# A planner's time for VectorE's instructions made a fourteenth longer, for ScalarE's a twenty-fifth

## The chip, the core and the metric

The kernel runs on one core of a Trainium2 chip. Its time is what one execution takes on the device, in microseconds; several executions are timed, and their median counts. One more execution is recorded by the hardware profiler, and all rows below are from that one.

## What is computed

Three layers follow one another on 4 batches of 768 tokens with 384 channels. The first is a gated linear attention with 8 heads of 48 channels; the second a gated network whose gate is mixed over the tokens; the third turns the channels by angles, mixes the tokens with two more 768 x 768 matrices and ends with a product over the channels.

```python
# layer 1, for each batch and head: state is 48 x 48, f = sigmoid(f_logit)
state = f[t][:, None] * state + outer(k[t], v[t])
y[t] = q[t] @ state
# layer 2
h = gelu_tanh(x @ w_in)
u, v = h[..., :512], h[..., 512:]
v_n = (v - mean(v)) / sqrt(var(v) + 1e-06) * g_ln
v_s = einsum('ts,bsd->btd', w_sg, v_n) + b_sg[None, :, None]
x = x + (u * v_s) @ w_out
# layer 3
theta = x @ w_theta
y = einsum('ts,bsd->btd', w_tok_r, x * cos(theta)) + einsum('ts,bsd->btd', w_tok_i, x * sin(theta))
u = x + y
out = u + maximum(u @ w_ch, 0)
```

The weights arrive as 64-bit floats, which the kernel reads as pairs of 32-bit integers.

## The kernel before

**Numbers in two parts.** A product in full float32 precision is made of three: each factor is split in a high part (fp32r) and the rest, and high x high, high x low and low x high are summed in one PSUM bank (lines 783, 784 and 785 of one helper, so all products have these three lines). ScalarE writes the high part and VectorE subtracts it to make the low part: L802 and L803 for the activations, L792 and L793 for a gated tile, L446 and L447 for a weight. Four PSUM banks (mm_95 to mm_98) serve these products, two more the attention (at).

**Decodes.** A 64-bit weight tile is loaded by SyncE (L420) into one of two raw buffers, ScalarE takes the absolute value of its upper word (L432), VectorE assembles the 32-bit float in four steps (L433 to L436), L446 and L447 split it, into one single buffer wt, and GpSimd issues its store to a scratch in DRAM (L483, scratch<-wt). Only when that store has landed can the next L446 write wt. The 24 tiles of the third layer's token mix are decoded so during the earlier layers; later SyncE streams them back (L493, st<-scratch) into five buffers. The channel weight w_ch is decoded in three parts into wmid, stored by L483 and loaded by L475 (win<-scratch) into the place of the input weights.

**Order of the work.** Batch by batch, layer 2 runs with the attention of the next batch between its products; layer 3 follows, the last batch first. In layer 2 the v tiles come first (products into a bank, gelu L958, mean L963 and L964, square L967, then for three tiles the power L979 on GpSimd, the scaling L987 on ScalarE and its low part L991 on VectorE), then u (gelu L828), the spatial gating (24 products into four banks at once, evicted by L846, multiplied by u in L851, split by L792 and L793) and the projection with w_out, whose sum is added in L807. The attention of a half batch needs a gate's seeds for four pairs of heads: a memset on GpSimd (L568), a scan on VectorE, the logarithm L583 and the exponential L584 on ScalarE; then for each pair transposes (L628), copies, the scores and the state updates (L681, L686) and a copy of the result (L733), which GpSimd's L756 sends to the next layer's input. Each change between ScalarE's sets of functions (gelu; logarithm and exponential; sine) takes a table load (L312).

**The planner.** No order is written by hand: every instruction is first put into a list with its engine, a planned duration, what it reads and writes and a due time vt. The planner makes each due time the least of its own and of its successors' due times less the planned cost, lets the engines run in a simulation and takes on each the ready instruction that is due first. The instructions are then emitted in that order, and each engine keeps it on the chip. The foreground's due times advance with the products; the decodes' are set apart by constants (LATE_AT, LATE_STEP). A duration is a line in the number n of columns, v1 for most VectorE operations, a1 for ScalarE's, and every additional engine waited for adds WAIT2:

```python
    def v1(n):
        return 0.069 + n * 0.00104

    def a1(n):
        return 0.1 + n * 0.00081
```

Of the kernel before, what the change touches and what calls it, by code (L numbers as in the profile page):

```python
# [65 lines left out]
LOOK = 0.05  # L66
SWITCH = 2.0
WAIT2 = 0.065

TICK = 10.24 / 3  # L70
DMA_SLACK = 1.0
# [43 lines left out]
class Plan:  # L115
# [17 lines left out]
    def op(self, eng, dur, fn, r=(), w=(), wp=(), table=None, dma=0, vt=None, cols=None):  # L133
        o = Op()
        o.eng, o.dur, o.fn, o.table, o.dma = eng, dur, fn, table, dma
        o.vt, o.n = self.vt if vt is None else vt, len(self.ops)
        o.cols = dur * 2400 if cols is None else cols
        deps, o.need = set(), []
        for b in r:
            deps.update(b.writers)  # L140
        for b in w:
            deps.update(b.writers)
        for b in (*w, *wp):
            deps.update(b.readers)
        for b in r:
            b.readers.append(o)
        for b in w:
            b.writers, b.readers = [o], []
        for b in wp:
            b.writers = b.writers + [o]  # L150
        for b in (*r, *w, *wp):
            root = b.of or b
            if root.slots is not None:
                if root not in o.need:
                    o.need.append(root)
                if not root.acc or root.acc[-1] is not o:
                    root.acc.append(o)

        o.dur += WAIT2 * max(0, len({d.eng + str(bool(d.dma)) for d in deps if d.eng != eng or d.dma}) - 1) * (eng in ("DVE", "ACT"))
        o.deps, o.succ, o.left = deps, [], len(deps)  # L160
        for d in deps:
            d.succ.append(o)
        self.ops.append(o)
        return o
# [159 lines left out]
def body(tc, ctx, att, qkv, flog, w_in, g_ln, w_sgT, b_sg, w_out, w_theta, w_rT, w_iT, w_ch, out):  # L324
# [87 lines left out]
    def load_f32(pl, g, d, src, vt, background=False):  # L412

        n = src.shape[-1]
        get = lambda: d.t[:, :n]
        if src.dtype != I64:
            dma(pl, "SP", n * 512, lambda: nc.sync.dma_start(get(), src), w=[d], vt=vt - 3)
            return
        raw = pl.buf(g.raw if background else g.st, [P, 2 * TH], I32)
        dma(pl, "SP", n * 1024, lambda: nc.sync.dma_start(raw.t[:, : 2 * n], src.bitcast(I32)), [], [raw], vt=vt - 3)  # L420

        def bits():
            r = raw.t[:, : 2 * n].rearrange("p (n two) -> p n two", two=2)
            return r[:, :, 0], r[:, :, 1]

        def op(dur, fn, eng="DVE"):
            pl.op(eng, dur, fn, [raw], [d], vt=vt)

        V, iget = nc.vector, lambda: get().bitcast(I32)


        op(a1(n), lambda: nc.scalar.activation(get(), bits()[1].bitcast(F32), AF.Abs), "ACT")  # L432
        op(v2(n), lambda: V.tensor_scalar(get(), get(), TINY, None, ALU.max))  # L433
        op(v2(n), lambda: V.tensor_scalar(iget(), iget(), 3, 0x3FFFFFFF, ALU.logical_shift_left, ALU.bitwise_and))
        op(v1(n), lambda: V.scalar_tensor_tensor(iget(), bits()[1], -0x40000000, iget(), ALU.bitwise_and, ALU.bitwise_or))  # L435
        op(v1(n), lambda: V.scalar_tensor_tensor(iget(), bits()[0], 29, iget(), ALU.logical_shift_right, ALU.bitwise_or))  # L436
# [801 lines left out]
```

## Time and profile before

| what | us |
|---|---|
| median of 3 timed runs | 668.9 |
| lowest and highest | 667.99, 669.65 |
| the profiled execution | 673.68 |
| its span, first to last instruction | 671.8 |
| TensorE busy in it | 615.1 |
| VectorE, ScalarE, GpSimd busy | 445.8, 355.9, 107.9 |

The mean clock granted to TensorE in the profiled execution is 0.982 of full speed. Times inside the program are counted from the start of its span. An engine's idle time costs something only where another engine, in the end TensorE, waits for it.

### The profile page before, as it was taken

Reading aid. Unit: us, or ns where it says so; the run is one execution under the profiler, and the core shown is the slowest. Engines: PE = TensorE matmul, PEld = TensorE weight load, DVE = VectorE, ACT = ScalarE, POOL = GpSimd, SP = SyncE. Lnnn points to the kernel's source line nnn. Section 1 sums busy time; section 2 is a strip of 40 time slices with the busy share of each in tenths; the row PEclk is TensorE's granted clock in tenths of the full one; section 3 lists DMA queues with packets and bytes.
Section 4 is the critical chain, followed back from the end, with each engine's and each line's share of the span. In section 5 each row is a group of like instructions: output and inputs, shape, how many; then the busy total and the mean of one; then the engine's idle time right before and its main releaser. Section 6 shows DMA issues by size and latency. Waiting matters only on the chain.

```text
span 671.8 us, 15019 instructions
## 1 busy us (share of the span) xinstructions
PE 615.1 (92%) x5963; PEld 566.7 (84%) x5963; DVE 445.8 (66%) x1029; ACT 355.9 (53%) x752; POOL 107.9 (16%) x202
## 2 busy tenths in 40 slices
PE   9788588799999999999989988999999999999996
PEld 8677477688888797888979888889989998998995
DVE  6999677979779988788765667932481175148203
ACT  6759596757795548855357234820390065029200
POOL 2001332153431432512313010000000000000000
PEclk9999878999999999999989999999999999999998
DMA  8531853478547684555764857188628844860862
GB/s 326 206 95 62 323 176 122 121 254 281 179 127 238 219 296 160 167 183 191 255 220 147 268 179 252 49 300 295 209 84 272 254 162 144 257 211 24 256 190 77
DMA packets 49296, 131.50 MB, mean 196 GB/s; under 512 B 6816, under 2 KB 17248, under 8 KB 48960
## 3 DMA queue, kind: packets, MB, share of 16 engines
q1 hardware_dynamic: 38656, 88.95, 41.0%
q0 software_dynamic: 10560, 41.49, 17.8%
q8 instruction: 49, 0.80, 0.5%
q14 instruction: 31, 0.25, 0.1%
HBM read 100.93 MB, written 24.77 MB: 187 GB/s over the span
## 4 chain that ended last, share of the span: by engine, by line
PE 31%; DVE 24%; ACT 19%; DMA 14%; issue 9%; POOL 2%; SPq 0%; DVEq 0%; POOLq 0%; ACTq 0%
PE mm L783 10%; PE mm L785 10%; PE mm L784 10%; DMA raw<-in_w_iT 3%; DMA scratch<-wt 3%; DVE dt L435 2%; DMA xst<-y 2%; DMA dt<-in_w_sgT 2%; ACT ar L792 2%; DVE s L681 2%; DVE dt L436 2%; DVE ar L793 2%; ACT tmp L964 1%; ACT junk L967 1%; ACT tmp L958 1%
## 5 line engine op out<-in xcount | busy, mean ns | idle before, releaser
L783 PE MATMUL mm<-st,ar 128*128 128x384 f32 x480 | 165.3, 344 | 4.6 <-DVE xst L807 2.3
L785 PE MATMUL mm<-st,ar 128*128 128x384 f32 x480 | 161.3, 336 | 0.0
L784 PE MATMUL mm<-st,ar 128*128 128x384 f32 x480 | 161.2, 336 | 0.0
L802 ACT CAST x<-xst 128x384 fp32r<-128x384 f32 x72 | 36.7, 512 | 150.5 <-DVE xst L807 126.6
L807 DVE TENSOR_TENSOR xst<-xst,mm 128x384 f32<-128x384 f32 x48 | 25.8, 551 | 109.9 <-PE mm L785 109.8
L783 PEld LDWEIGHTS mm<-st,ar 128*128 128x128 f32 x480 | 90.5, 189 | 8.7 <-DVE xst L807 3.0
L784 PEld LDWEIGHTS mm<-st,ar 128*128 128x128 f32 x480 | 90.6, 189 | 0.3
L785 PEld LDWEIGHTS mm<-st,ar 128*128 128x128 f32 x480 | 90.5, 189 | 0.0
L783 PE MATMUL mm<-win,x 128*128 128x512 f32 (+1 forms) x144 | 56.0, 389 | 8.8 <-DVE tmp L846 4.0
L783 PE MATMUL mm<-x,win 128*128 128x384 f32 x168 | 58.9, 351 | 3.1 <-DVE tmp L846 1.8
L785 PE MATMUL mm<-x,win 128*128 128x384 f32 x168 | 56.8, 338 | 0.8 <-DVE win L447 0.8
L785 PE MATMUL mm<-win,x 128*128 128x512 f32 (+1 forms) x144 | 53.7, 373 | 3.8 <-DVE x L803 3.8
L784 PE MATMUL mm<-x,win 128*128 128x384 f32 x168 | 56.6, 337 | 0.0
L784 PE MATMUL mm<-win,x 128*128 128x512 f32 (+1 forms) x144 | 53.4, 371 | 0.1
L793 DVE TENSOR_TENSOR ar<-tmp,ar 128x384 fp32r<-128x384 f32 x80 | 41.2, 553 | 4.3 <-ACT ar L792 3.8
L792 ACT CAST ar<-tmp 128x384 fp32r<-128x384 f32 x80 | 37.7, 508 | 12.0 <-DVE tmp L851 11.1
L803 DVE TENSOR_TENSOR x<-xst,x 128x384 fp32r<-128x384 f32 x72 | 37.5, 553 | 4.4 <-ACT x L802 3.1
L783 PEld LDWEIGHTS mm<-win,x 128*128 128x128 f32 x144 | 27.4, 190 | 14.2 <-DVE tmp L846 5.3
L783 PE MATMUL mm<-ar,wout 128*128 128x384 f32 x96 | 34.6, 360 | 2.0 <-DVE tmp L898 1.8
L783 PEld LDWEIGHTS mm<-x,win 128*128 128x128 f32 x168 | 31.8, 189 | 5.1 <-DVE tmp L846 2.4
L756 POOL DMA_DIRECT2D xst<-y x60 | 30.8, 518 | 26.3 <-ACT y L733 17.1
L785 PEld LDWEIGHTS mm<-win,x 128*128 128x128 f32 x144 | 27.6, 191 | 7.4 <-DVE x L803 4.4
(146 smaller groups left out, 1238.4 us busy)
## 6 DMA issues: line engine op xcount, KB each, us to landing
st<-scratch SPq DMA_DIRECT2D x132, 384.0 KB, 3.8
qkv<-in_qkv POOLq DMA_DIRECT2D x24, 536.0 KB, 5.5
scratch<-wt POOLq DMA_DIRECT2D x24, 384.0 KB, 3.9
f<-in_flog POOLq DMA_DIRECT2D x6, 768.0 KB, 5.2
scratch<-st POOLq DMA_DIRECT2D x12, 384.0 KB, 6.8
raw<-in_w_rT SPq DMA_DIRECT2D x12, 384.0 KB, 4.1
raw<-in_w_iT SPq DMA_DIRECT2D x12, 384.0 KB, 4.9
out<-xst SPq DMA_DIRECT2D x24, 192.0 KB, 2.2
```

What stands on the lines that cost most here:

```text
L435: op(v1(n), lambda: V.scalar_tensor_tensor(iget(), bits()[1], -0x40000000, iget(), ALU.bitwise_and, ALU.bitwise_or))
L436: op(v1(n), lambda: V.scalar_tensor_tensor(iget(), bits()[0], 29, iget(), ALU.logical_shift_right, ALU.bitwise_or))
L681: pl.op("DVE", 0.16, lambda: V.tensor_add(s1(), s0(), U(c)), r=[ps, b0], w=[b1])
L756: lambda r0=r0, n=n, kc=kc, o=64 * j + off: q[yq].dma_start(xst.t[r0 : r0 + n, kc], y.t[o : o + n].rearrange("p i a t -> p (i a t)")),
L783: nc.tensor.matmul(o, h0, h1, start=start, stop=False)
L784: nc.tensor.matmul(o, h0, l1, start=False, stop=False)
L785: nc.tensor.matmul(o, l0, h1, start=False, stop=stop)
L792: pl.op("ACT", a1(n), lambda: nc.scalar.copy(tiles()[0], src.t[:, :n]), [src], [hi])
L793: pl.op("DVE", v1(n), lambda: V.tensor_sub(tiles()[1], src.t[:, :n], tiles()[0].bitcast(F32)), [src, hi], [lo])
L802: pl.op("ACT", a1(TH), lambda: nc.scalar.copy(X[hf][:, 0, k], T()), [src], [hi])
L803: pl.op("DVE", v1(TH), lambda: V.tensor_sub(X[hf][:, 1, k], T(), X[hf][:, 0, k].bitcast(F32)), [src, hi], [lo])
L807: pl.op("DVE", v1(TH), lambda: V.tensor_add(T(), T(), ps.t[:, :TH]), [ps], [xst[hf].parts[k]])
```

## The change

The planner multiplies every planned duration of VectorE by 1.07 and of ScalarE by 1.04. Nothing else is edited; the same operations are emitted, in another order on each engine.

```diff
 SWITCH = 2.0
 WAIT2 = 0.065
 
+
+SLOW = {"DVE": 1.07, "ACT": 1.04}
+
 TICK = 10.24 / 3
@@ -157,6 +160,7 @@
         o.dur += WAIT2 * max(0, len({d.eng + str(bool(d.dma)) for d in deps if d.eng != eng or d.dma}) - 1) * (eng in ("DVE", "ACT"))
+        o.dur *= SLOW.get(eng, 1.0)
         o.deps, o.succ, o.left = deps, [], len(deps)
```

Of VectorE's planned instructions 633 of 1016 stand elsewhere, by up to 61 places; of ScalarE's 359 of 689, of GpSimd's 84 of 193, of SyncE's 88 of 272. ScalarE's planned part holds 17 table loads, where it held 15. From line 70 on, the changed kernel's lines have numbers higher by 3, from line 160 on by 4: L846 is L850 there.

GpSimd during batch 1's first attention, 94 to 140 us. L979 is the power of layer 2's statistics, L568 the memset of the next half's seeds. Before:

```order
L491 DMA scratch_91<-st_1172 128x768
L963 TENSOR_SCALAR stat_875<-stat_875 128x1 x3
L539 DMA f_1265<-in_flog 128x1536
L979 TENSOR_TENSOR stat_875<-stat_875,mhalf 128x3
L568 MEMSET seed_1311 128x1536
L491 DMA scratch_91<-st_1294 128x768
```

After:

```order
L495 DMA scratch_91<-st_1186 128x768
L967 TENSOR_SCALAR stat_887<-stat_887 128x1 x3
L543 DMA f_1317<-in_flog 128x1536
L572 MEMSET seed_1330 128x1536
L983 TENSOR_TENSOR stat_887<-stat_887,mhalf 128x3
L495 DMA scratch_91<-st_1319 128x768
```

The power and the memset have changed places.

ScalarE during batch 3's attention in the middle of the run. L583 and L584 are the logarithm and the exponential of the seeds, L828 the gelu of u, L987 the scaling of three v tiles. Before:

```order
L828 ACTIVATE u_3820<-mm_97 128x384
L828 ACTIVATE u_3825<-mm_96 128x384
L312 ACT_TABLE_LOAD
L583 ACTIVATE seed_3469<-f_3491 128x1536
L733 COPY y_3881<-at_99 128x2x3x64
L691 ACTIVATE s_3865<-s_3865,bends 128x48 x2
L691 ACTIVATE carry_3902<-s_3865,bends 128x48
L584 ACTIVATE seed_3469<-seed_3469 128x1536
L312 ACT_TABLE_LOAD
L828 ACTIVATE u_3916<-mm_95 128x384
```

After:

```order
L832 ACTIVATE u_3767<-mm_96 128x384
L737 COPY y_3771<-at_100 128x2x3x64
L695 ACTIVATE s_3760<-s_3760,bends 128x48 x2
L316 ACT_TABLE_LOAD
L587 ACTIVATE seed_3537<-f_3553 128x1536
L991 ACTIVATE ar_0_3820<-tmp_3617,stat_3496 128x512
L991 ACTIVATE ar_0_3820<-tmp_3695,stat_3496 128x512
L991 ACTIVATE ar_0_3820<-tmp_3707,stat_3496 128x512
L695 ACTIVATE carry_3837<-s_3760,bends 128x48
L636 ACTIVATE kt_3842<-at_100 128x384
L316 ACT_TABLE_LOAD
L832 ACTIVATE u_3849<-mm_97 128x384
```

The three scalings, a transpose's copy (L632, now L636) and the gelus have come between the logarithm and the exponential, with a table load before and one after them; the exponential (L588) follows seven rows further down, behind one more load.

VectorE at the spatial gating of batch 2's second half, 335 to 348 us. L846 evicts one of its four banks, L851 and L793 multiply and split; L433 to L436 and L447 belong to a decode. L1101 belongs to the test of the decays. Before:

```order
L846 SCALAR_TENSOR_TENSOR tmp_4566<-mm_98,gcol,bbc 128x384
L851 TENSOR_TENSOR tmp_4566<-tmp_4566,u_4169 128x384
L793 TENSOR_TENSOR ar_0_4561<-tmp_4548,ar_0_4561 128x384
L447 TENSOR_TENSOR wt_4572<-dt_4323,wt_4572 128x384
L793 TENSOR_TENSOR ar_0_4561<-tmp_4566,ar_0_4561 128x384
L433 TENSOR_SCALAR dt_4584<-dt_4584 128x384
L434 TENSOR_SCALAR dt_4584<-dt_4584 128x384
L435 SCALAR_TENSOR_TENSOR dt_4584<-raw_4481,dt_4584 128x384
L436 SCALAR_TENSOR_TENSOR dt_4584<-raw_4481,dt_4584 128x384
L846 SCALAR_TENSOR_TENSOR tmp_4610<-mm_97,gcol,bbc 128x384
L1101 TENSOR_REDUCE lmin<-lps 1x1
L851 TENSOR_TENSOR tmp_4610<-tmp_4610,u_4196 128x384
```

After:

```order
L797 TENSOR_TENSOR ar_0_4563<-tmp_4546,ar_0_4563 128x384
L440 SCALAR_TENSOR_TENSOR dt_4540<-raw_4478,dt_4540 128x384
L850 SCALAR_TENSOR_TENSOR tmp_4580<-mm_96,gcol,bbc 128x384
L855 TENSOR_TENSOR tmp_4580<-tmp_4580,u_4163 128x384
L850 SCALAR_TENSOR_TENSOR tmp_4596<-mm_97,gcol,bbc 128x384
L850 SCALAR_TENSOR_TENSOR tmp_4604<-mm_98,gcol,bbc 128x384
L855 TENSOR_TENSOR tmp_4596<-tmp_4596,u_4179 128x384
L797 TENSOR_TENSOR ar_0_4563<-tmp_4580,ar_0_4563 128x384
L855 TENSOR_TENSOR tmp_4604<-tmp_4604,u_4266 128x384
L451 TENSOR_TENSOR wt_4578<-dt_4374,wt_4578 128x384
L797 TENSOR_TENSOR ar_0_4563<-tmp_4596,ar_0_4563 128x384
```

The second, third and fourth eviction now stand ahead of the decode's L447 (now L451), and its four steps come later still. At the next spatial gating, near 382 us, one L447 and four decode steps stand right before the four evictions in both orders.

SyncE loads the third part of w_ch five places later, behind four more stream loads L493, and on TensorE 57 products of the last batch's token mix stand ahead of the first product with w_ch, where there were 42.

## Rows read from the trace of the kernel before

**Rows 1.** Busy time of each engine in six stretches of the span, whole kernel.

```profile
core 0: us, PE busy (x) PEld busy (x) DVE busy (x) ACT busy (x) POOL busy (x), PEclk, DMA share, GB/s
0.00:94.00 94.00, 75.74 (x1116) 65.80 (x1117) 77.69 (x221) 68.08 (x152) 15.32 (x37) 0.93 0.55 191
94.00:140.00 46.00, 38.94 (x623) 33.42 (x622) 40.17 (x99) 28.69 (x58) 14.24 (x23) 0.96 0.45 141
140.00:341.00 201.00, 192.97 (x2490) 170.13 (x2489) 164.94 (x378) 130.26 (x266) 65.66 (x118) 1.00 0.67 219
341.00:359.00 18.00, 14.73 (x69) 13.24 (x68) 12.57 (x29) 12.05 (x27) 5.00 (x10) 0.91 0.42 143
359.00:430.00 71.00, 64.29 (x360) 61.35 (x359) 47.54 (x99) 35.46 (x77) 6.02 (x12) 1.00 0.57 193
430.00:672.00 242.00, 228.44 (x1314) 222.79 (x1312) 102.91 (x209) 81.34 (x173) 1.61 (x3) 0.99 0.60 193
```

**Rows 2.** What TensorE waited for: us in total, times, longest us.

```profile
PE at L628 <- ACT y L733: 6.7, 5, 2.2
...
PE mm L783 <- DVE tmp L846: 5.8, 6, 3.3
```

**Rows 3.** The costliest groups of instructions, page part 5: busy, mean ns of one.

```profile
L802 ACT CAST x<-xst 128x384 fp32r<-128x384 f32 x72 | 36.7, 512 | 150.5 <-DVE xst L807 126.6
L807 DVE TENSOR_TENSOR xst<-xst,mm 128x384 f32<-128x384 f32 x48 | 25.8, 551 | 109.9 <-PE mm L785 109.8
```

**Rows 4.** GpSimd's timeline, 93 to 98 us: start, us.

```profile
94.35 1.12 POOL L979 TENSOR_TENSOR stat<-stat,mhalf 128x3 f32<-128x3 f32 x1 [1.80 <-DVE stat L974]
95.44 1.37 POOL L568 MEMSET seed<- 128x1536 f32 x1
```

**Rows 5.** The chain that ended last, around 100 and 450 us: start, us, what.

```profile
100.46 5.93 DMA st<-in_w_out
...
444.17 8.79 DMA scratch<-wmid
...
453.02 6.41 DMA win<-scratch
```

**Rows 6.** TensorE's timeline at six places; in brackets its idle time before.

```profile
111.72 0.33 PE L628 MATMUL at<-ident,qkv 128*128 128x128 f32 x1 [2.10 <-ACT y L733]
...
346.13 0.50 PE L783 MATMUL mm<-win,x 128*128 128x512 f32 x1 [3.27 <-DVE tmp L846]
...
382.94 0.44 PE L783 MATMUL mm<-x,win 128*128 128x384 f32 x1 [1.54 <-DVE tmp L846]
...
434.21 0.44 PE L783 MATMUL mm<-st,ar 128*128 128x384 f32 x1
...
453.29 0.41 PE L783 MATMUL mm<-st,ar 128*128 128x384 f32 x1 [1.61 <-DMA st<-scratch]
...
459.57 0.41 PE L783 MATMUL mm<-x,win 128*128 128x384 f32 x1 [1.32 <-DMA win<-scratch]
```

**Rows 7.** The table loads of ScalarE, L312: count and ns of one.

```profile
L312 ACT ACT_TABLE_LOAD  x15: 1283/1283/1283, 0.8 to 416.5; - x15
```

**Rows 8.** VectorE's timeline, 338 to 384 us, three instructions.

```profile
342.40 0.56 DVE L447 TENSOR_TENSOR wt<-dt,wt 128x384 fp32r<-128x384 f32 x1 [3.60 <-ACT wt L446]
...
345.47 0.61 DVE L846 SCALAR_TENSOR_TENSOR tmp<-mm,gcol,bbc 128x384 f32<-128x384 f32 x1
...
379.22 0.56 DVE L447 TENSOR_TENSOR wt<-dt,wt 128x384 fp32r<-128x384 f32 x1 [3.77 <-ACT wt L446]
```

**Rows 9.** ScalarE's timeline at 342 us.

```profile
341.85 0.51 ACT L446 CAST wt<-dt 128x384 fp32r<-128x384 f32 x1 [4.57 <-DMA scratch<-wt]
```

**Rows 10.** Busy time and granted clock (PEclk) of 348 to 351 us.

```profile
348.00:351.00 3.00, 3.00 (x10) 2.71 (x10) 0.56 (x2) 2.94 (x8) 0.60 (x1) 0.51 1.01 400
```

**Rows 11.** SyncE's queue, 436 to 450 us: nine stream loads.

```profile
438.19 10.88 SPq L493 DMA_DIRECT2D st<-scratch  x9
```

**Rows 12.** DMA issues, page part 6: KB each, median us to landing.

```profile
st<-scratch SPq DMA_DIRECT2D x132, 384.0 KB, 3.8
...
raw<-in_w_iT SPq DMA_DIRECT2D x12, 384.0 KB, 4.9
```

## Prediction

> **What bounds the kernel now.** I read the table of stages first: it cuts the span where the work changes and gives each engine's busy time in each piece. TensorE works 615.1 of 671.8 us and is idle for 56.9, of which 18.3 us lie in the first 94 us, 7.1 in 94 to 140, 8.0 in 140 to 341, 3.3 in 341 to 359, 6.7 in 359 to 430 and 13.6 after that [rows 1]. The change adds and removes no product, so TensorE's 615 us stay; what it can win is a part of these 56.9 us and of the time at the lower clock, and what it can lose is new waiting. Next I read what ended TensorE's waits: six waits for the eviction L846 of a spatial-gating bank make 5.8 us, one of them 3.3; five for the attention's copy L733 make 6.7 [rows 2]. Then, for the places where those waits stand, the timelines and the chain.
>
> **Is the new cost nearer the truth?** A VectorE operation on 384 columns is planned at 0.069 + 384 x 0.00104 = 0.468 us; times 1.07 that is 0.501. The trace has 551 ns for L807, which is such an operation. A ScalarE operation on 384 columns is planned at 0.1 + 384 x 0.00081 = 0.411 us, after the change 0.428, and the trace has 512 ns for L802 [rows 3]. So both move towards what the chip does and stay short of it. Only the order of the instructions can follow from this. Due times are worked backward with these costs, so a foreground chain (evict, multiply, split) becomes due earlier, and the decodes of later weights, whose due times are given, slip behind it. I compared the two orders place by place and price five stretches.
>
> **Start, 0 to 94 us.** The attention of batch 0 comes a little ahead of the decode of the input weights, the rest is the same order on an engine that is dense here: VectorE works 77.7 of these 94 us [rows 1]. I put -0.3 us, bounds -1 and +1: the gate that opens the rest can move by a decode step or two of half a us each.
>
> **94 to 140 us, batch 1's first attention.** On GpSimd the power L979 (1.12 us from 94.35) and the memset L568 (1.37 us from 95.44) change places [rows 4]. The power now comes at least 1.37 us later; if the memset starts where it starts today, because what frees its buffer is no earlier, the power ends 1.37 + 1.12 after 95.44, at 97.9 against 95.5, 2.5 us later. Behind the power stand ScalarE's scaling L987, VectorE's L991 and the last spatial-gating products, and what frees their weight buffer releases SyncE's load of the output weights. That load is in the chain: 5.93 us from 100.46, then ScalarE's decode step, a table load, two functions and the copy L733, until TensorE goes on at 111.72 after 2.10 us idle [rows 5, 6]. So I carry the delay to the end of that chain: +2.2 us, between +0.5 (the memset could run in the gap before the power, and the chain has some slack) and +4 (two evictions L846 are also put behind the attention's chain on VectorE). Nothing of ScalarE's is free here to hide it: the copy waits for the two functions, and those for the load.
>
> **140 to 341 us.** Decodes slip by up to 20 us; with them out of its way the attention of batches 2 and 3 should wait less. But TensorE loses only 8.0 of 201 us here, in many waits of under 1.5 us [rows 1], and ScalarE is given two more table loads, 15 before and 17 after, at 1283 ns each [rows 7], because three scalings and three gelus now stand between the logarithm and the exponential of the seeds. I put -0.5, between -4 (half of the 8.0 us) and +4 (two loads of 1.28 us, with a copy L733 held up behind them as in the 2.10 us of [rows 6]).
>
> **341 to 430 us, the gain.** The large wait is at 346.13: 3.27 us, for L846 [rows 6]. VectorE stood for 3.60 us at a decode's L447, until 342.40; only after it, behind one more split and four decode steps, came the eviction, at 345.47 [rows 8]. L447 waited for ScalarE's L446 at 341.85, which itself had waited 4.57 us for the store of the one decoded-weight buffer [rows 9]. TensorE had filled those banks when its idleness began, at 346.13 - 3.27 = 342.86. After the change the four evictions stand in one piece ahead of that L447, and the two v tiles take their banks as soon as the last products have left them. TensorE then also does not fall to the lower clock: after the 3.27 us of idleness it was granted 0.51 of full speed over 348 to 351 [rows 10], 1.2 in place of 2.4 GHz, which cost about half of 3.0, 1.5 us. Together 4.8 us. Against it: the projection that follows needs the splits of all four tiles, and ScalarE's hi splits two to four still stand behind L446 and behind a v tile's gelu and statistics. L446 comes at 341.85 as now, since the store before it is not earlier; the hi split of the second tile follows at 342.3, the gelu and its two followers take about 2.5 us with GpSimd's step between, and the third and fourth are done near 346; TensorE, which would ask for the third at about 346.2, waits some 0.5 us. So 4.3.
>
> The second place is 382.94. There VectorE stood 3.77 us at another L447 until 379.22, and the evictions came behind four decode steps more [rows 8]; TensorE waited 1.54 us for them [rows 6], which with the 3.27 is most of the 5.8 [rows 2]. The order around it is the same after the change, one decode fewer has gone ahead; the three decodes before it come at the same places among the gelus and scalings. So its wait stays, or grows where TensorE, now 4.3 us earlier, meets the pace of the stores, which allow a decode every 5 to 7 us. I put +0.3 for it. The stretch is worth -4.0, between -7 (both waits go) and 0 (see the second rival).
>
> **430 us to the end.** The last decodes and the channel weight slip. SyncE's third raw load of the channel weight goes behind four stream loads. Nine of these took 10.88 us from 438.19 [rows 11], so the fifth place is reached about 4 x 1.2 = 4.8 us after 438.2, at 443.0, 8.8 us after the token mix began at 434.2 [rows 6]. The raw load takes 4.9 [rows 12]; its decode I estimate at 3.5, seven operations in a row of about the 0.5 us of [rows 3]; then come the store of 8.79 and the load of 6.41 us [rows 5]: 434.2 + 8.8 + 4.9 + 3.5 + 8.79 + 6.41 = 466.6. Before, the product that needs it was reached at 459.57 - 1.32 = 458.25 [rows 6]; in the new order fifteen products of three matmuls are moved ahead of it, 57 in place of 42, at about 0.52 us each (24.05 us less the 1.61 of waiting for the 42 are 0.53), 7.8 us. The wait of 1.61 was for a stream load, of which five that followed SyncE's waiting load now stand ahead of it; with it gone the product is reached at 458.25 - 1.6 + 7.8 = 464.4 and waits 2.2. The waits of today are 1.61 + 1.32 = 2.9. So -0.7, between -3 (the store finds emptier queues) and +7 (the fourth rival). From about 480 us on the order is nearly the same as before.
>
> **Sum.** -0.3 + 2.2 - 0.5 - 4.0 - 0.7 = -3.3 us. The profiled execution took 673.68 us, with a span of 671.8, and stands 4.8 us above the median of the timed runs, 668.9; the differences are worked out in the one and taken off the other: 665.6 us. Timed runs of this kernel lie 1.7 us apart, so about 0.3%, 2 us, is what a measurement can tell from no change.
>
> A rule speaks against the change. The trace has 15 table loads of 1283 ns, and the time behind each is not seen as work on ScalarE [rows 7]. The Trainium skill, page "ScalarE: Activation LUTs", section "What ACT_TABLE_LOAD costs", agrees on the 1283 ns and adds some 1380 ns of draining for each switch; by it an estimate of the two more switches is 5.3 us of ScalarE's time in place of 2.6. Its section on table sets says that functions of one set belong together, and the new order parts them.
>
> **The rivals.** (1) The middle gains too: the postponed decodes free VectorE in 140 to 341 us, and the waits there halve, -4.0 in place of -0.5, with 1 us less at 94 to 140. For it: VectorE works 165 of 201 us and ScalarE 130 [rows 1], so decodes do hold the foreground up. Against it: the waits are short and have many causes. 668.9 - 0.3 + 1.2 - 4.0 - 4.0 - 0.7 = 661.1.
> (2) The wait moves and does not go: the decodes are the same in number with one buffer, and each must be stored before the next is split. If the pace of the stores is what binds from 341 to 383 us, what is won at 346 is waited for at 383, where L447 at 379.22 already waits 3.77 us [rows 8]. Then the stretch is worth 0 and the sum +0.7: 669.6.
> (3) The table loads: 2 x 1.28 = 2.6 us come in the path of the attention's copy, +2.5 in place of -0.5 for the middle: 668.6. The rule of the Trainium skill named above, page "ScalarE: Activation LUTs", would give this, or more.
> (4) The other side: the channel weight comes late. If its third raw load takes as long as the store of today, 8.79 in place of 4.9, the product waits 2.2 + 3.9 = 6.1 us, and the stream loads queued behind SyncE's waiting load come 3.8 us [rows 12] later: 9.9 against 2.9, +7.0 in place of -0.7: 668.9 - 2.6 + 7.0 = 673.3. It decides from the point where these two waits pass 2.9 + 2.6 + 2 = 7.5 us. For it: SyncE, its queue and the store are in a row; against: three of the last weights' loads of today are hidden.
>
> **How the numbers follow.** My forecast 0.46 (its own range 661.5 to 669), rivals (1) 0.13, (2) 0.18, (3) 0.09, (4) 0.14. The likeliest is 665.6. Faster by over 0.3% means under 666.9: 0.32 of my forecast's 0.46, all of (1), 0.05 of (2) and 0.02 of (4): 0.52. Within 0.3%, to 670.9: 0.12 of the forecast, 0.08 of (2), 0.07 of (3), 0.01 of (4): 0.28. Slower: 0.02 + 0.05 + 0.02 + 0.11 = 0.20. A range of 659.5 to 673 leaves out the lower third of (1), half of (4) and the ends of the rest, under 0.2.
>
> **What would show it.** Right: in 335 to 350 us VectorE's four evictions close behind TensorE's last products, no idle of 3 us at the v tiles and no granted clock of one half there; at about 97 us the power later by 1.4 to 2.5 us, the load of the output weights later by about as much; 17 table loads. Wrong, if the wait before the evictions at the next spatial gating grows by what is saved, if the chain at 111.7 is no later, since then it has cover that I do not see, or if TensorE stands over 5 us at its first product with the channel weight.

## The result and the profile after

The changed kernel takes 679.99 us (median; 675.29 to 684.99) against 669.27 us for the kernel before: a ratio of 1.0135, with a 95% interval of 1.0095 to 1.0175, so about 9 us slower where 3.3 us less were forecast. The profiled execution took 679.86 us with a span of 678.2; its mean granted clock is 0.972, against 0.982 before.

The table of stages of the kernel after, cut as in [rows 1]; its columns are the stretch, its length, the busy time of TensorE, its weight loads, VectorE, ScalarE and GpSimd with counts, the granted clock, the DMA share and GB/s:

```profile
0.00:94.00 94.00, 77.17 (x1134) 66.88 (x1134) 76.73 (x213) 66.92 (x149) 14.45 (x36) 0.93 0.53 189
94.00:140.00 46.00, 37.30 (x560) 33.12 (x561) 37.24 (x95) 28.88 (x60) 11.03 (x18) 0.89 0.43 135
140.00:341.00 201.00, 195.46 (x2544) 173.25 (x2543) 163.34 (x375) 130.21 (x264) 69.59 (x122) 0.99 0.65 207
341.00:359.00 18.00, 16.28 (x83) 14.61 (x82) 11.79 (x26) 11.13 (x27) 3.62 (x8) 1.00 0.66 222
359.00:430.00 71.00, 63.68 (x347) 60.70 (x346) 48.77 (x101) 36.00 (x79) 7.64 (x15) 0.98 0.59 203
430.00:679.00 249.00, 233.54 (x1332) 227.00 (x1330) 108.57 (x222) 84.13 (x178) 2.17 (x4) 0.98 0.59 191
...
sum 679.00, PE 623.42 PEld 575.56 DVE 446.44 ACT 357.27 POOL 108.50; mean PE 103.90 PEld 95.93 DVE 74.41 ACT 59.54 POOL 18.08
```

TensorE's idle time did not grow: 678.2 - 623.4 = 54.8 us, against 56.9 in [rows 1]. What grew is the busy time, 623.4 against 615.1 us: in part the same work at a lower granted clock, in part eleven more warming products (products whose results nothing uses) ahead of the first v tile. A loss can so stand in the busy column. But stages cut at fixed times hold different work in the two traces, so I matched them by the start of the same product instead. The first v tile of batch 0 starts at 47.49 us (45.82 before, +1.7); a product in that batch's first gating at 95.66 (93.79, +1.9) and the last tile of its first projection at 140.81 (135.20, +5.6); batch 2's last gating at 326.6 (322.5, +4.1); batch 3's u products at 363.2 (362.3, +0.9), its second projection at 391.0 (388.2, +2.8), its second set of angles at 429.7 (426.0, +3.7); the last products at 670.9 (664.5, +6.4). The table of stages of the kernel before, and then of the kernel after, for the worst of these stretches:

```profile
93.79:135.20 41.41, 34.35 (x578) 29.20 (x578) 35.65 (x89) 28.08 (x56) 10.31 (x17) 0.96 0.47 148
```
```profile
95.66:140.81 45.15, 36.45 (x577) 31.96 (x576) 36.56 (x92) 27.91 (x56) 11.61 (x19) 0.89 0.43 138
```

The same products take 3.7 us longer: 1.6 us more idle (7.1 to 8.7) and 2.1 us more busy, the clock at 0.89 in place of 0.96.

**Where it waits there.** The waits of TensorE after (engine and line, for whom: us in total, times, the longest), to be set beside [rows 2]; each line number of after is that of before plus 4:

```profile
PE at L632 <- ACT y L737: 8.7, 5, 4.2
PE mm L787 <- DMA st<-scratch: 4.0, 3, 2.4
PE mm L787 <- DVE tmp L850: 3.7, 3, 1.7
PE mm L787 <- ACT u L832: 3.5, 2, 1.8
```

The waits for the gating's eviction fell from 5.8 to 3.7 us, as forecast; those for the attention's copy rose from 6.7 to 8.7. GpSimd's timeline of after at the place of [rows 4] (start, us, engine, line, operation, in brackets the idle time before and what ended it):

```profile
96.73 0.59 POOL L543 DMA_DIRECT2D f<-in_flog  x1 [5.31 <-DVE stat L978]
97.33 1.40 POOL L572 MEMSET seed<- 128x1536 f32 x1
98.68 0.91 POOL L983 TENSOR_TENSOR stat<-stat,mhalf 128x3 f32<-128x3 f32 x1
```

Memset and power have changed places as forecast, and the power starts 4.33 us later, at 98.68 in place of 94.35; 1.9 us of this is the shift of the whole stretch, so that the rest is about the 2.5 that were forecast. But another delay stands a row above: the load of the gate f. It was issued at 91.95 before and is issued at 96.73 here, because VectorE's timeline has the last reader of the f before it behind seven instructions of scores and states:

```profile
94.10 0.21 DVE L681 COPY s<-at 128x48 f32<-128x48 f32 x1 [1.68 <-PE at L653]
...
95.88 0.55 DVE L617 TENSOR_TENSOR seed<-seed,f 128x384 f32<-128x384 f32 x1
```

L617 (L613 before) now stands behind a copy that waits for TensorE. The load comes 0.30 us behind its end, as it did before (0.29); the bracket names L978, which ended between the two. ScalarE's timeline of after shows who waits for it, and a second wait of its own:

```profile
104.06 1.49 ACT L573 ACTIVATE f<-f 128x1536 f32<-128x1536 f32 x1 [2.50 <-DMA f<-in_flog]
...
106.97 0.46 ACT L737 COPY y<-at 128x384 f32<-128x384 f32 x1
...
108.85 1.00 ACT L436 ACTIVATE dt<-st 128x384 f32<-128x384 f32 x2
...
124.79 0.51 ACT L806 CAST x<-xst 128x384 fp32r<-128x384 f32 x1 [2.65 <-DMA xst<-y]
125.21 0.51 ACT L796 CAST ar<-tmp 128x384 fp32r<-128x384 f32 x1
125.74 1.28 ACT L316 ACT_TABLE_LOAD   x1
127.03 0.49 ACT L832 ACTIVATE u<-mm 128x384 f32<-128x384 f32 x1
...
131.01 0.49 ACT L737 COPY y<-at 128x384 f32<-128x384 f32 x1
```

At 104 the functions of f wait for that load, and the copy L737 stands behind them. At 108.85 the decode steps of the output weights no longer wait; ScalarE's timeline of the kernel before had its wait there:

```profile
106.41 0.58 ACT L432 ACTIVATE dt<-st 128x384 f32<-128x384 f32 x1 [3.37 <-DMA st<-in_w_out]
```

At 124.79 the x split of the next tile, which has slipped ahead of the gating's splits, waits 2.65 us for a transfer; a table load, the gating's splits, gelus of u, the splits of three output weights and again the copy L737 stand behind it, and TensorE's timeline has the longest wait of the table:

```profile
131.56 0.43 PE L632 MATMUL at<-ident,qkv 128*128 128x128 f32 x1 [4.17 <-ACT y L737]
...
346.55 0.50 PE L787 MATMUL mm<-win,x 128*128 128x512 f32 x1 [1.72 <-DVE tmp L850]
...
372.60 0.45 PE L787 MATMUL mm<-st,ar 128*128 128x384 f32 x1 [1.85 <-ACT u L832]
...
466.36 0.69 PE L787 MATMUL mm<-st,ar 128*128 128x384 f32 x1 [2.36 <-DMA st<-scratch]
```

The other rows answer to [rows 6]: the 3.27 us at 346.13 are 1.72 now; 1.85 us for a gelu of u (L832) at 372.60 are new, with a granted clock of 0.80 over 371 to 376; and at the end the stream's loads come late.

### The profile page after: what moved, and what is told of

Read it like the earlier page. It is cut to its first block, busy times and chain, and to the rows that moved or that the text cites. A ratio compares the mean times of both kernels' runs of the same rounds, so it can differ in the third digit from the quotient of the medians.

```text
span 678.2 us, 15073 instructions
## 1 busy us (share of the span) xinstructions
PE 623.4 (92%) x5991; PEld 575.6 (85%) x5991; DVE 446.4 (66%) x1029; ACT 357.3 (53%) x754; POOL 108.5 (16%) x202
## 5 line engine op out<-in xcount | busy, mean ns | idle before, releaser
L787 PE MATMUL mm<-st,ar 128*128 128x384 f32 x480 | 167.7, 349 | 9.1 <-DMA st<-scratch 4.0
L788 PE MATMUL mm<-st,ar 128*128 128x384 f32 x480 | 163.2, 340 | 0.0
L789 PE MATMUL mm<-st,ar 128*128 128x384 f32 x480 | 163.2, 340 | 0.0
L806 ACT CAST x<-xst 128x384 fp32r<-128x384 f32 x72 | 36.7, 513 | 150.4 <-DVE xst L811 119.5
L787 PEld LDWEIGHTS mm<-st,ar 128*128 128x128 f32 x480 | 92.2, 192 | 14.1 <-ACT u L832 4.3
L788 PEld LDWEIGHTS mm<-st,ar 128*128 128x128 f32 x480 | 92.1, 192 | 0.3
L789 PEld LDWEIGHTS mm<-st,ar 128*128 128x128 f32 x480 | 92.0, 192 | 0.0
L789 PE MATMUL mm<-win,x 128*128 128x512 f32 (+1 forms) x144 | 53.3, 370 | 3.3 <-DVE x L807 3.3
L807 DVE TENSOR_TENSOR x<-xst,x 128x384 fp32r<-128x384 f32 x72 | 37.8, 553 | 8.0 <-ACT x L806 7.3
L787 PEld LDWEIGHTS mm<-win,x 128*128 128x128 f32 x144 | 27.4, 190 | 13.9 <-DVE tmp L850 3.7
L787 PE MATMUL mm<-ar,wout 128*128 128x384 f32 x96 | 34.9, 363 | 1.8 <-DVE tmp L902 1.8
L788 PE MATMUL mm<-ar,wout 128*128 128x384 f32 x96 | 33.2, 346 | 0.4 <-DVE ar L797 0.4
```

Of the source, the lines that this page charges most:

```text
L787: nc.tensor.matmul(o, h0, h1, start=start, stop=False)
L788: nc.tensor.matmul(o, h0, l1, start=False, stop=False)
L789: nc.tensor.matmul(o, l0, h1, start=False, stop=stop)
L806: pl.op("ACT", a1(TH), lambda: nc.scalar.copy(X[hf][:, 0, k], T()), [src], [hi])
L807: pl.op("DVE", v1(TH), lambda: V.tensor_sub(X[hf][:, 1, k], T(), X[hf][:, 0, k].bitcast(F32)), [src, hi], [lo])
```

## The experiments

Two tools serve most of them. In a hybrid the planner runs twice over the same list, with the factors ("slow") and without ("plain"); the emitted order is the one's until a named product of TensorE, and from there the other's for all that is left. Products 361, 537, 575, 1450 and 2199 stand at about 47, 108, 140, 322 and 410 us. In a local edit, named operations are put ahead of another one in the finished order. Every hybrid and edited kernel computes all that the kernel before does. Ratios are to the kernel before on the same chip, five rounds, with 95% intervals; 0.1% is 0.67 us. They stand in the order of the forecasts above them. An edited kernel has line numbers of its own, higher than those of before by a constant that is given with its rows.

**Which part of the program loses?**

```diff
+PIECES = [("slow", 575), ("plain", None)]     # new_then_old_140
+PIECES = [("plain", 575), ("slow", None)]     # old_then_new_140
+PIECES = [("plain", 1450), ("slow", None)]    # old_then_new_322
+PIECES = [("plain", 2199), ("slow", None)]    # old_then_new_410
```

> The changed order up to batch 0's second spatial gating (about 140 us), the order of before from there on. Theory 'places': the traces of before and after, matched product by product, put +1.7 us into the first 47 us and +3.5 us into 94 to 140 us, so this kernel takes about 5 us more than before, near 674.5 us, in all its runs. Rival 'tail': the order costs little anywhere, the loss and the wide spread (675 to 685 us) come from the last decodes and the channel weight alone; then this one is within 2 us of before.

> The order of before up to 140 us, the changed order from there on. 'Places': -2.1 us for 140 to 341, -3.3 for the v tiles at 346, +2.9 for 359 to 430, +2.5 for the end: 0, about 669 us. 'Tail': the whole loss is here, 675 us or more, and the spread is wide.

> The order of before up to batch 2's second spatial gating (about 322 us), the changed order from there on. 'Places': -3.3 + 2.9 + 2.5 = +2.1, about 671 us. 'Tail': 675 us or more.

> The order of before up to the first angles of batch 3 (about 410 us), the changed order from there on. 'Places': +2.5, about 671.5 us. 'Tail': 675 us or more.

Measured: 1.0108 [1.0065, 1.0150]; 0.9998 [0.9977, 1.0018]; 1.0026 [0.9998, 1.0055]; 1.0001 [0.9975, 1.0027]. 'Places' holds and 'tail' falls. The new order of the first 140 us alone carries the loss; the whole new order after it is worth nothing that can be measured, and a gain above 0.23% (1.5 us) there is outside the interval.

**Is it one of the three displacements seen in the trace?** On the changed kernel, L617 is put back ahead of the state updates, the power ahead of the memset, the x split behind the gating's, and all three together.

```diff
+MOVES = [([712], 656)]                               # new_l617_early
+MOVES = [([434], 739)]                               # new_power_first
+MOVES = [([837], 530)]                               # new_l806_late
+MOVES = [([712], 656), ([434], 739), ([837], 530)]   # new_three_back
```

> The changed kernel with one VectorE instruction put back: the product seed x f of the fourth pair in batch 1's first half stands again right behind the other preparations of that half, ahead of the seven state updates. Theory 'last reader': this product is the last to read f; put late it holds GpSimd's load of the next f (issued 4.8 us later), behind which the memset and the power stand, and ScalarE waits 2.5 us for the load with the copy behind it. Then the power comes back by some 2.5 us and the kernel wins 2 to 4 us on the changed one, to about 677. Rival 'swap': the exchange of power and memset on GpSimd is the cause and this product is not; then no change, 680.

> The changed kernel with the power ahead of the memset again on GpSimd, nothing else. 'Swap' (the step of the prediction): 2.2 us less than the changed kernel, about 677.5. 'Last reader': the load of f ahead of both still comes 4.8 us late; the power gains the memset's 1.4 us at most and nothing of it reaches the end, 679 to 680.

> The changed kernel with one ScalarE instruction put back: the high split of the second attention tile of batch 1 stands again behind the four gated tiles' splits, the three output weights and the four gelus. In the changed kernel's trace ScalarE stands 2.65 us at it, waiting for the attention's result from DRAM, and the copy behind it comes 5.1 us late (TensorE idle 4.17 us). Theory 'in line behind a wait': 2 to 3 us less, about 677.5. Rival: the copy waits for the evictions on VectorE, which are also late; then under 1 us.

> All three together. If these three places are the cause of the loss in 94 to 140 us: 5 us less than the changed kernel, near 674 to 675, of which the first 47 us keep +1.7 and the end +2. If the loss is of another kind (a spread that any new order brings): 679 to 681 as before.

Measured: 1.0114 [1.0072, 1.0156]; 1.0131 [1.0087, 1.0175]; 1.0088 [1.0056, 1.0120]; 1.0116 [1.0077, 1.0154], against 1.0135 for the change itself. None gives back much, and none can be told from the change itself: a difference of two such ratios is known to within 0.5 or 0.6%. The x split may be worth half a per cent, but its interval overlaps the change's; that the three make up most of the loss, 5 us, is not borne out by these times. Whether the power's place matters, a forecast of 2.2 us, these times cannot say; ScalarE's timeline of new_power_first can (line numbers higher by 22 than those of before):

```profile
98.38 1.94 ACT L1009 ACTIVATE ar<-tmp,stat 128x512 fp32r<-128x512 f32 x3
103.24 1.49 ACT L591 ACTIVATE f<-f 128x1536 f32<-128x1536 f32 x1 [2.93 <-DMA f<-in_flog]
```

The scalings behind the power are done by 100.3, and ScalarE still waits for the load of f: with that load late, the power's place does not decide when the copy comes. The profiles leave one thing open. From the last of batch 0's first six v gelus (L958) to the first sum of its projection (L807) after takes 48.8 us, the kernel before 45.3, new_three_back 43.9; so the three repairs may have mended this stretch, with the loss elsewhere. But eight profiles with the old order there spread from 41.8 to 45.4, and single profiles prove no more.

**Which piece of the first 140 us?**

```diff
+PIECES = [("slow", 361), ("plain", None)]                    # new_until_47
+PIECES = [("plain", 361), ("slow", 575), ("plain", None)]    # new_47_to_140
+PIECES = [("plain", 537), ("slow", 575), ("plain", None)]    # new_108_to_140
+PIECES = [("plain", 361), ("slow", 537), ("plain", None)]    # new_47_to_108
```

> The changed order until the first v tile (about 47 us), the order of before from there on. The three local repairs in 94 to 140 us brought 1 to 3 us of the 10 that the changed first 140 us cost, so most of it must stand elsewhere before 140 us. Theory 'start': batch 0's attention and the first weights cost the most, +5 us or more here, 675 or above, and with a wide spread. Rival 'gating': the loss stands between 47 and 140 us; then +1.7 at most, 671 to 672.

> The order of before, with the changed order only from the first v tile to batch 0's second gating. 'Start': 1 to 4 us over before, 671 to 674. 'Gating': 677 or more.

> The order of before, with the changed order only from batch 0's second half of u (about 108 us) to its second gating. The high split that ScalarE waits at stands here: +2 us by the trace, 672. If nothing of the loss stands here: 670.

> The order of before, with the changed order only from the first v tile to batch 0's second half of u (47 to 108 us); the late product that holds the load of f, and 13 more warming products, stand here. 'Gating': the rest of the loss, 675 or more. 'Start': 670 to 673.

Measured: 1.0035 [1.0009, 1.0062]; 1.0091 [1.0061, 1.0121]; 1.0055 [1.0028, 1.0082]; 1.0093 [1.0064, 1.0122]. Each piece loses by itself; 'start', which gave the first piece 5 us or more, falls, and 'gating' holds. They do not add: 108 to 140 us costs 0.55% alone, 47 to 108 us 0.93%, and the two together 0.91%. I take it that work late by one delay is not late again by the next; no run shows this. Nor was a seam run by itself: what it costs to change from one order to the other at 47 or 108 us is not known (at 140 and 410 us seam and new order together cost nothing that can be measured).

**The late reader alone, the mended piece, and the gain alone.** In the kernel before, the last reader of f and the gate's load (712, 734) are put where the new order has them. In the hybrid of 47 to 108 us, L617 and the power are put back. And in the kernel before, the decodes around 346 us (15 operations, and nine more at 382) are put behind the gating's evictions.

```diff
+MOVES = [([712, 734], 433)]                          # old_l613_late
+for ops, target in (((712,), 656), ((434,), 739)):   # new_47_to_108_mended
+MOVES = [([2062, 2063, 2083, 2084, 2085, 2086, 2087, 2100], 1492),   # old_346_evictions
+    ([2070], 1489), ([2071, 2072, 2092], 2093), ([2079, 2080, 2101], 2102)]
+    ([2107, 2108, 2128, 2129, 2130, 2131, 2132, 2145], 1830), ([2115], 1844)   # and old_346_382_evictions
```

> The kernel before with one product put late: seed x f of the fourth pair (L613) behind the seven state updates, and GpSimd's load of the next f with it, as in the changed order; the power stays ahead of the memset. 'Last reader': the load of f comes 3 us later, ScalarE waits for it with the copy behind: +2 to +4 us, 673 to 674. Rival: the order of before absorbs it; 670 to 671.

> The kernel with the changed order from 47 to 108 us alone (which took 0.93% more than before), with the early product and the power ahead of the memset put back. 'Last reader': the larger part goes, 0.2 to 0.4% over before remain. Rival 'many places': another cause in 47 to 108 us keeps 0.7% or more.

> The kernel before with the evictions at 346 us put ahead of the decode's L447 and its four steps, and the three decodes behind it one place later; the start is that of before. By the prediction's term: the wait of 3.27 us and the lower clock go, -3 to -4 us, 666.5. Rival 'the wait moves': the stores' pace binds, the gating at 382 us gives it back: 0, 670.

> The same with the evictions at 382 us ahead of their decode too. By the term: -4.5 to -5.5 us, 665. 'The wait moves': the later decodes, and with them the channel weight, come late and the end gives it back: -1 to +1.

Measured: 1.0050 [1.0021, 1.0079]; 1.0099 [1.0064, 1.0134]; 1.0013 [0.9985, 1.0042]; 1.0057 [1.0029, 1.0085]. The late reader alone makes the old kernel half a per cent slower, as 'last reader' forecast. ScalarE's timeline of that run (numbers higher by 18) shows its first step, the wait for the load of f, with the copy behind it:

```profile
99.56 1.48 ACT L587 ACTIVATE f<-f 128x1536 f32<-128x1536 f32 x1 [1.07 <-DMA f<-in_flog]
...
102.47 0.46 ACT L751 COPY y<-at 128x384 f32<-128x384 f32 x1
...
106.22 0.55 ACT L450 ACTIVATE dt<-st 128x384 f32<-128x384 f32 x1 [1.35 <-DMA st<-in_w_out]
...
111.00 0.46 ACT L751 COPY y<-at 128x384 f32<-128x384 f32 x1
```

It does not show the rest of the way. The copy comes at 102.47 in place of 100.64, but the wait for the output weights is 2.0 us shorter than before (1.35 against 3.37), and the next copy comes at 111.00 against 111.21; this one profile ends up at a span of 671.0, under the 671.8 of before. So the half per cent rests on the timed runs, and where it arises is not shown.

To put the late reader back in the new order gives nothing that can be measured (1.0099 against 1.0093, 'many places'): in the profiles of the two hybrids the copy comes at 102.61 in place of 106.13, and yet the first sum of the projection (L807) at 136.27 and 136.21. So other obstacles hold the same chain there. In the run with the evictions of 346 us put ahead (numbers higher by 21), they come early, as VectorE's timeline says, but TensorE's has another wait in that place, and the wait of the next gating as before:

```profile
341.56 0.62 DVE L867 SCALAR_TENSOR_TENSOR tmp<-mm,gcol,bbc 128x384 f32<-128x384 f32 x1 [0.52 <-PE mm L806]
...
342.87 0.60 DVE L867 SCALAR_TENSOR_TENSOR tmp<-mm,gcol,bbc 128x384 f32<-128x384 f32 x1
```
```profile
349.18 0.45 PE L804 MATMUL mm<-ar,wout 128*128 128x384 f32 x1 [1.46 <-ACT ar L813]
...
381.94 0.44 PE L804 MATMUL mm<-x,win 128*128 128x384 f32 x1 [1.56 <-DVE tmp L867]
```

ScalarE's timeline there:

```profile
348.22 0.49 ACT L467 CAST wt<-dt 128x384 fp32r<-128x384 f32 x1
348.62 0.92 ACT L813 CAST ar<-tmp 128x384 fp32r<-128x384 f32 x2
...
377.68 0.51 ACT L467 CAST wt<-dt 128x384 fp32r<-128x384 f32 x1 [5.25 <-DMA scratch<-wt]
```

The 3.27 us at 346 are gone, 1.46 come back three microseconds on for ScalarE's split L813 (L792 before), the wait at 382 is as before (1.56, and 1.54 then), and the timed runs see no gain; one above 0.15% (1.0 us) is outside the interval. The split stands behind a v tile's gelu and statistics and behind a decode's L467 (L446), which did not wait for its store here; at 377.68 it did, for 5.25 us. With the second place mended too the kernel is slower by 0.57%, which neither text forecast.

**The warming products.** The planner fills the longer pause that it plans ahead of the first v tile with 14 warming products in place of 3.

```diff
+out[i] = ((14, out[i][0][1]), None)    # old_14_warm, in the kernel before
+out[i] = ((3, out[i][0][1]), None)     # new_47_to_108_3_warm, in new_47_to_108_mended
```

> The kernel before with 14 warming products ahead of the first v tile's first product, where it has 3, as the changed order has there (their results are used by nothing). In the traces 14 last from 44.3 to 47.7 us, and the first product, whose inputs came at 45.8 in the old order, starts at 47.5 to 48.1. Theory 'filled gap': +1.5 us, 671.5 to 672. Rival: the tile waits for its inputs anyway; 670.

> The kernel with the changed order in 47 to 108 us alone, the late product and the power put back (0.99% over before), now with 3 warming products in place of the 14 ahead of the first v tile. 'Filled gap': the larger part of the 0.99% goes, 0.2 to 0.5% remain. 'Many places': 0.7% or more remain.

Measured: 1.0009 [0.9978, 1.0039] and 1.0062 [1.0029, 1.0095]. In the kernel before they cost nothing that can be measured, though the forecast of +1.5 us (0.22%) lies inside the interval; without them the hybrid stands at 1.0062 in place of 1.0099, with overlapping intervals. Neither theory is decided by this. What is left of the hybrid's loss is not one place that I could name. The timelines of VectorE and TensorE in new_47_to_108_3_warm (numbers higher by 72) have a candidate that was not tried: the low parts of three scaled v tiles (L991 of before, L995 of after) are put behind state updates whose first copy waits for TensorE.

```profile
99.87 0.21 DVE L749 COPY s<-at 128x48 f32<-128x48 f32 x1 [2.50 <-PE at L721]
...
101.64 2.07 DVE L1063 SCALAR_TENSOR_TENSOR ar<-tmp,stat,ar 128x512 fp32r<-128x512 f32 x3
```
```profile
114.03 0.33 PE L700 MATMUL at<-ident,qkv 128*128 128x128 f32 x1 [2.76 <-ACT y L805]
```

## Why the prediction was wrong, step by step

**What bounds the kernel:** right. TensorE's time is the kernel's. But I counted what the change can win or lose as idle time, with the clock priced at one place alone; in the profile of after, whose span is 6.4 us longer, TensorE is idle 2.1 us less and busy 623.4 - 615.1 = 8.3 us more, at a mean clock of 0.972 in place of 0.982.

**"Start, 0 to 94 us" (-0.3, bounds -1 and +1): failed.** The first v tile starts 1.7 us later in the trace, and the new order up to 47 us alone is timed at +0.35% (2.3 us, by its interval 0.6 to 4.2), for the most part outside the bounds. The start of the first product alone is a poor mark: in old_14_warm, with 14 warming products ahead of it, it comes at 48.16, and yet the first gelu of a v tile (L958) at 53.97. That gelu starts at 53.3 to 54.7 us in eight profiles whose start is that of before, and at 54.7 to 57.1 in the seven with the new start. In three of these seven the granted clock of the first 47 us is 0.93 to 0.96; it is 1.00 in the other four, after among them, and in all 13 profiles with the old order up to 47 us. So the profile of after does not show all of this loss. I had called it "the same order on an engine that is dense here"; that a dense engine has no gap in which a step out of place could vanish is my reading of it, and no run shows it.

**"94 to 140 us" (+2.2, bounds +0.5 and +4): the step that decided, and it failed in cause and size.** The swap that I described is there, but the path along which I carried its delay is not: from the power over the scalings and the last gating products to the load of the output weights, and from that load to the copy. After the change ScalarE does not wait for that load at all (3.37 us before); what holds the copy is the load of f, for which it waits 2.50 us, and 2.93 us with the power put first again. With the swap undone the time is 1.0131 in place of 1.0135, within the noise. What the same comparison of orders showed and I left without a price is VectorE's L613, the last reader of a single buffer, behind a waiting copy: alone it costs 0.50% (0.21 to 0.79). The new order of 47 to 140 us is timed at +0.91% (6.1 us); the trace has 3.7 us after 94 us. Of the bound of +4 I said that two evictions are also put behind the attention's chain; I looked for operations that come later, not for ones that come earlier and wait, as the x split L806 does. How the rest of the 0.9% divides among single places stays open.

**"140 to 341 us" (-0.5):** about -1.5 in the trace (+5.6 to +4.1), in timed runs not to be told from nothing. The 17 table loads came as forecast. ScalarE's timeline at 125 us above shows what a switch costs: 1.28 us for the load, and the function behind it starts at 127.03, with 0.01 us between. The same holds in the kernel before (load at 107.01, function at 108.30), so at these two switches the time behind a load, of which the prediction speaks, is nothing. The rule of the Trainium skill, page "ScalarE: Activation LUTs", section "What ACT_TABLE_LOAD costs", agrees on the 1283 ns; the 1380 ns of draining that it adds are not seen here. Rival (3), a loss of 2.5 us here, did not come.

**"341 to 430 us, the gain" (-4.0, bounds -7 and 0): mechanism right in place, wrong in worth.** VectorE's timeline of after has the evictions as forecast, close together with no decode's L451 ahead:

```profile
344.47 0.56 DVE L807 TENSOR_TENSOR x<-xst,x 128x384 fp32r<-128x384 f32 x1 [1.02 <-ACT x L806]
...
345.88 0.61 DVE L850 SCALAR_TENSOR_TENSOR tmp<-mm,gcol,bbc 128x384 f32<-128x384 f32 x1
...
347.01 1.14 DVE L850 SCALAR_TENSOR_TENSOR tmp<-mm,gcol,bbc 128x384 f32<-128x384 f32 x2
```

Yet they do not follow TensorE's last products at once. The low part L807 and, at 345.42, one step of a decode stand ahead of them, and L807 waited for the x split L806, which by ScalarE's timeline had waited 1.85 us for its transfer, until 343.93: the same kind of wait as at 124.79. So 1.72 of the 3.27 us stay. The clock stays at 1.00 over 341 to 359, with no fall to 0.51 as in [rows 10], and up to the u products 3.2 us are won (+4.1 to +0.9). By 391 us 1.9 of them are lost again, by 430 us 2.8. So far this is rival (2), to which I gave 0.18: the wait moves and does not go. The experiment on the old kernel shows it with hardly anything else changed: 1.0013. But the reason that rival (2) gives, the pace of the stores, is seen at the gating of 382 us alone, whose wait stays as it was. The waits that are new stand on ScalarE: 1.46 us at 349.18 in that experiment for a split behind a v tile's gelu and statistics, and 1.85 us at 372.60 in after for a gelu of u, ahead of which ScalarE works without a gap from 363.34 (1.60 and 1.84 us in old_then_new_140 and old_then_new_322). The prediction has the first of them, as "some 0.5 us"; that term was too small by about a microsecond, and the second is not in the sum.

**"430 us to the end" (-0.7, bounds -3 and +7):** +2.7 in the trace, nothing that can be told from zero in timed runs (1.0001). The channel weight's product did not wait, so rival (4) was wrong; the stream loads behind SyncE's waiting load were late, as it says: SyncE's timeline has the load of the channel weight at 466.20 (453.02 in [rows 5]), and a granted clock of 0.57 behind it in the table of stages.

```profile
466.20 0.57 SPq L479 DMA_DIRECT2D win<-scratch  x1
466.88 3.08 SPq L497 DMA_DIRECT2D st<-scratch  x2
```
```profile
466.00:470.00 4.00, 3.64 (x12) 3.64 (x13) 0.00 (x0) 0.00 (x0) 0.00 (x0) 0.57 0.86 292
```

**The sum.** After 140 us I forecast -0.5 - 4.0 - 0.7 = -5.2, and 0 was timed; before it +1.9, and +1.08% (7.2 us) was timed. So the gain was given back, and the loss was more than three times its forecast. Two things stay open. From the last tile of batch 0's first projection to the first token-mix product of layer 3 the new order takes 294.6 to 297.1 us in six profiles and the old 296.9 to 304.3 in ten, some 4 us less by the means; from there to the end 238.6 to 240.3 against 236.7 to 238.4, 2 us more. The 2 us that are left the timed runs do not show. And the two factors were not run apart, so whether VectorE's or ScalarE's makes the bad start is not known. No version beat the kernel before.

## What to carry to other kernels

A cost that comes nearer to the chip's own need not make the order better; here it made it 1.35% worse. Where a place could be named, an instruction waited and others stood in line behind it. So in a comparison of orders look first at the densest stretch, for two kinds: the last reader of a buffer of which there is one, now behind a waiting instruction, and an instruction whose input comes by DMA, now ahead of others. And before a removed wait is booked as a gain, ask who is next in line: here the next products waited for a split in ScalarE's queue, and the next gating for a store as before. Single profiles of one order differ by some 3 us in one stretch (41.8 to 45.4 above), so smaller effects take timed rounds.

## What the runs showed of the hardware

While GpSimd cleared a seed of 128x1536, VectorE's operations with a tensor and a scalar stood still until it was done. VectorE's timeline of after has the same line twice, and GpSimd's has the memset from 25.95 to 27.33:

```profile
24.42 0.16 DVE L561 TENSOR_SCALAR ar<-ar 128x3 f32<-128x3 f32 x1
...
26.21 1.14 DVE L561 TENSOR_SCALAR ar<-ar 128x3 f32<-128x3 f32 x1
```
```profile
25.95 1.38 POOL L572 MEMSET seed<- 128x1536 f32 x1 [20.65 <-DVE bends L611]
```

In the traces of before, after and old_then_new_140 all 7 that overlapped such a memset took 1.11 to 1.27 us in place of 0.16 to 0.36; the 36 operations on two tensors that overlapped one were not lengthened. (Beside the four memsets of 128x384 at the start, 0.38 us each, one such operation in each of the three traces took 0.17 to 0.22 us.) The Trainium skill, page "GPSIMD Engine Reference", section "1. Specifications", names both kinds, VectorE's two-port modes and its instructions with two SBUF inputs, as contending with GpSimd. The traces here show a stall for operations with one tensor input, whose mode no trace shows, and none for those with two, against a memset, which reads nothing.
